# A range test's last step put between two matmul groups, and its result tile allocated ahead of the weights

## The chip, the core and the metric

The kernel runs on one core of a Trainium2 chip. The metric is the device time of one execution in microseconds (us). The kernel before took 517.93 us, the median of three runs (517.24 to 519.18). The execution that the profiler recorded took 517.73 us; its span, from the first to the last instruction, is 516.0 us.

## The reference

The inputs are q, k and v of 4 batches, 8 heads, 768 positions and 64 values a head, two sizes (8 global and 96 local positions), and weights of a feed-forward part that come as float64 numbers. The core of the reference:

```python
scores = scale * np.matmul(q, k.transpose(0, 1, 3, 2)) + bias   # bias falls with the distance
scores = np.where(is_global | is_local, scores, -1e9)
a = np.exp(scores - scores.max(-1, keepdims=True)); a /= a.sum(-1, keepdims=True) + 1e-9
x = np.matmul(a, v)                            # heads joined: (4, 768, 512)
xk = mu_k * x + (1 - mu_k) * x_prev            # x_prev: x one position earlier
xr = mu_r * x + (1 - mu_r) * x_prev
k = np.maximum(xk @ w_k, 0)
out = 1 / (1 + np.exp(-(xr @ w_r))) * (k * k @ w_v)
```

## The kernel before

The rows are cut into 24 tiles of 128 positions. For each tile the kernel makes the scores (tile `s`), the exponentials (`e`), their transposes (`t`, `et`) and the weighted sums (`av`). Two tiles make a chunk of 256 positions for the feed-forward part, of which there are 12. A chunk runs as a generator, `channel_mix`, that the main loop advances by some matmuls at a time, so that TensorE has feed-forward matmuls between the attention's. Each product with a weight is made of three float32r matmuls (`three`, lines 440 to 442), because operands are held as a high and a low part. The groups are `kp` (weights `wk` stationary, 256 columns of `xk` moving; 1152 matmuls), `z` (`xr` stationary, 512 columns of `wr` moving; 288) and `vps` (`kk` stationary, 512 columns of `wv` moving; 576). A chunk ends with two `vps` groups of 24 matmuls. After each of them VectorE multiplies by the sigmoid (line 489) and SyncE issues the write of 128 rows of the output (line 490).

The weights come as 64-bit words and are turned into float32 by bit operations, which hold for a range of exponents only. The kernel therefore loads all weights again in the last two chunks (`range_load`) and tests their exponents (`range_test`): 20 tests, each of which leaves one number per partition in a column of `odd`. At the end, in program order after all chunks, line 554 takes the largest of the 20 columns into `worst[:, 0]`, line 556 turns this column into one row by a product with the identity (`row`), line 557 takes the largest of the row into `worst[0, 1]`, and lines 692 and 693 make of it a flag, `wide_i`. All five engines load the flag into a register (line 695) and branch (line 696). The flag is 0 for these inputs; the branch then leaps over `wide()`, a slow version for all other inputs, to the end of the program. What all engines do from there to the end stands at lines 696 and 738: waits on the DMA counters, resets of semaphores and a barrier.

All tiles of the pool `const` lie one behind the other in the order in which the program allocates them: among others `odd`, `middle`, `k_first`, the ten weight tiles of 8192 bytes per partition (`w0` to `w9`), `worst`, `okf`, `wide_i`. The other pools lie behind it. The pool of the second phase's operands has gaps written in by hand (`GAP`, and the tile `ahead`, which nothing uses), of 64, 448 and 384 bytes per partition.

The order of the instructions on each engine is set by a scheduler that models the time of each; only the order within a queue matters to this case. PSUM tiles of the feed-forward part (`kp`, `z`, `vps`, `row`) share three buffers in turn.

Of the kernel before, what the change touches and what calls it, by code (L numbers as in the profile page):

```python
# [9 lines left out]
F32 = mybir.dt.float32  # L10
# [6 lines left out]
AX = mybir.AxisListType  # L17
# [24 lines left out]
def tile_biased_attention_channel_mix(ctx: ExitStack, tc: tile.TileContext, qT, kT, v, n_sizes, mu_kr, w_k, w_v, w_r, q_rows, k_rows, v_rows, slopes, out):  # L42
    nc = tc.nc
    vec, act, pool, pe = nc.vector, nc.scalar, nc.gpsimd, nc.tensor

    const = ctx.enter_context(tc.tile_pool(name="const", bufs=1))
# [14 lines left out]
    ident = const.tile([128, 128], F32, name="ident")  # L61
# [26 lines left out]
    ps_f = fast.enter_context(tc.tile_pool(name="ps_f", bufs=3, space=PSUM))  # L88
# [108 lines left out]
    words_again, tested = [], [0]  # L197

    def range_load():
        n = len(words_again)  # L200
        if n == 20:
            return
        name, src, j = w_steps[n // 2]
        if n % 2:
            raw = p4k.tile([128, 512, 2], I32, tag="t4k", name=f"again_{n}")
        else:
            raw = q_pool.tile([128, 512, 2], I32, tag=("qh", "ql")[n // 2 % 2], name=f"again_{n}")
        at, o = divmod((j * 2 + n % 2) * 512 // 512 * 1024 + n % 1 * 1024, 2048 if name == "k" else 1024)
        nc.sync.dma_start(raw.rearrange("p n w -> p (n w)"), src[at * 128 : (at + 1) * 128, o : o + 1024])
        words_again.append(raw)  # L210

    def range_test(behind_vec, behind_act):
        n = tested[0]
        if n == len(words_again):
            return
        tested[0] += 1
        raw = words_again[n]
        low, top = raw[:, :, 0], raw[:, :, 1]
        with tc.issue_after(behind_vec.ins):
            vec.tensor_scalar(low, top, 27, 15, op0=ALU.logical_shift_right, op1=ALU.bitwise_and)  # L220
        with tc.issue_after(behind_act.ins):
            act.activation(top.bitcast(F32), low, AF.Abs, bias=middle, accum_out=odd[:, n : n + 1])

    odd = const.tile([128, 20], F32, name="odd")
    middle = const.tile([128, 1], F32, name="middle")
    pool.memset(middle, -7.5)

# [16 lines left out]
    def weights_need(n):  # L244
        weights_go(n, n)
# [172 lines left out]
    def part(pool, tag, n):  # L418
        t = pool.tile([128, n * 256 + GAP.get(tag, 0)], F32R, name=tag, tag=tag)
        return t[:, 0 : n * 256].rearrange("p (a q) -> p a q", a=n)  # L420
# [15 lines left out]
    def channel_mix(xk, xr, out_rows, f_pool, f2_pool, ps_f, more=False):  # L436
        kkh, kkl = (part(f_pool, f"kk_{p}", 8) for p in ("hi", "lo"))

        def three(o, sh, sl, mh, ml, first, last):
            pe.matmul(o, sh, mh, start=first, stop=False)  # L440
            pe.matmul(o, sh, ml, start=False, stop=False)  # L441
            pe.matmul(o, sl, mh, start=False, stop=last)  # L442

        def z_of(i):
            z = ps_f.tile([128, 512], F32, name="z", tag="f")
            c = slice(i * 128, (i + 1) * 128)
            for k in range(4):
                three(z, xr[0][:, k, c], xr[1][:, k, c], *wts["r", k], k == 0, k == 3)
                yield
            sig = f2_pool.tile([128, 512], F32, name="sig", tag="f2")  # L450
            sigs.append((z, sig))

        sigs = []
        for fp in range(4):
            weights_need(4)
            ps = ps_f.tile([128, 512], F32, name="kp", tag="f")
            for u in range(2):
                f = slice((2 * fp + u) * 128, (2 * fp + u + 1) * 128)
                o = ps[:, u * 256 : (u + 1) * 256]
                for k in range(4):  # L460
                    hi, lo = wts["k", k]
                    three(o, hi[:, f], lo[:, f], xk[0][:, k, :], xk[1][:, k, :], k == 0, k == 3)
                    if k % 2:
                        yield
            kk = f2_pool.tile([128, 2, 256], F32, name="kk", tag="f2")
            pv = ps.rearrange("p (a q) -> p a q", a=2)
            act.activation(kk, pv, AF.Relu)  # L467
            vec.tensor_mul(kk, pv, kk)  # L468
            high = act.copy(kkh[:, 2 * fp : 2 * fp + 2, :], kk)  # L469
            rest = vec.tensor_sub(kkl[:, 2 * fp : 2 * fp + 2, :], kk, kkh[:, 2 * fp : 2 * fp + 2, :])  # L470
            if more:
                for i in range(3):
                    range_load()
                for i in range(3):
                    range_test(rest, high)
        weights_need(6)
        for i in range(2):
            yield from z_of(i)
        for z, sig in sigs:
            act.activation(sig, z, AF.Sigmoid)  # L480
        for i in range(2):
            c = slice(i * 128, (i + 1) * 128)
            vp = ps_f.tile([128, 512], F32, name="vps", tag="f")
            sig = sigs[i][1]
            for f in range(8):
                weights_need(7 + f // 2)
                three(vp, kkh[:, f, c], kkl[:, f, c], *wts["v", f], f == 0, f == 7)
                yield
            vec.tensor_mul(sig, vp, sig)
            nc.sync.dma_start(out_rows(i), sig)  # L490

    def ffn(c):
        xt = state["x", c]
        xk = mix(xt[:, :, 1:257], xt[:, :, 0:256], "k", p4k, f_pool, c == 0)
        xr = mix(xt[:, :, 1:257], xt[:, :, 0:256], "r", p4k, f_pool, c == 0)
        return channel_mix(xk, xr, lambda i: out[(2 * c + i) * 128 : (2 * c + i + 1) * 128, :], f_pool, f2_pool, ps_f, c >= 10)
# [53 lines left out]
    while queue:  # L550
        run_ffn(1.0)
    assert tested[0] == 20
    worst = const.tile([128, 2], F32, name="worst")
    vec.reduce_max(worst[:, 0:1], odd, axis=AX.X)
    row = ps_f.tile([128, 512], F32, name="row", tag="f")
    pe.matmul(row[0:1, 0:128], worst[:, 0:1], ident, start=True, stop=True)
    vec.reduce_max(worst[0:1, 1:2], row[0:1, 0:128], axis=AX.X)
    fast.close()


# [16 lines left out]
    def wide():  # L577
        weights_any()
        with ExitStack() as g:
# [85 lines left out]
            with tc.For_i(0, B, 1) as b:  # L665
                for c in range(3):
                    xt = work.tile([128, 4, 257], F32, name="g_x", tag="g_x")
                    src = rows[ds(b, 1)].rearrange("b p a s -> p (b a) s")
                    if c:
                        nc.sync.dma_start(xt, src[:, :, 256 * c - 1 : 256 * c + 256])  # L670
                    else:
                        pool.memset(xt[:, :, 0:1], 0.0)
                        nc.sync.dma_start(xt[:, :, 1:257], src[:, :, 0:256])
                    xk = mix(xt[:, :, 1:257], xt[:, :, 0:256], "k", work, work)
                    xr = mix(xt[:, :, 1:257], xt[:, :, 0:256], "r", work, work)

                    def out_rows(i):
                        return rows_out[ds(b, 1), (2 * c + i) * 128 : (2 * c + i + 1) * 128, :].rearrange("b s d -> (b s) d")

                    for _ in channel_mix(xk, xr, out_rows, work, work4, ps_f):  # L680
                        pass
# [60 lines left out]
```

## Time and profile before

| | |
|---|---|
| three runs | 517.24, 517.93, 519.18 us |
| profiled execution | 517.73 us, span 516.0 us |
| TensorE busy | 503.1 us (98%) |
| VectorE, ScalarE, GpSimd busy | 344.8, 345.8, 220.4 us |
| mean granted TensorE clock | 0.984 of 2.4 GHz |
| data moved | 59.95 MB, 116 GB/s on average |

A page of the profile gives busy time by engine (PE is TensorE's matmuls, PEld its weight loads, DVE is VectorE, ACT ScalarE, POOL GpSimd, SP SyncE). An engine name with a q behind it (SPq, DVEq) is the engine's sequencer, which waits, branches, loads registers and issues DMAs. Matmuls are pipelined: the time from one matmul's start to the next one's start is the pace, and the duration in a row is longer than that.

### The profile page before, as it was taken

Reading aid. Unit: us, or ns where it says so; the run is one execution under the profiler, and the core shown is the slowest. Engines: PE = TensorE matmul, PEld = TensorE weight load, DVE = VectorE, ACT = ScalarE, POOL = GpSimd, SP = SyncE. Lnnn points to the kernel's source line nnn. Section 1 sums busy time; section 2 is a strip of 40 time slices with the busy share of each in tenths; the row PEclk is TensorE's granted clock in tenths of the full one; section 3 lists DMA queues with packets and bytes.
Section 4 is the critical chain, followed back from the end, with each engine's and each line's share of the span. In section 5 each row is a group of like instructions: output and inputs, shape, how many; then the busy total and the mean of one; then the engine's idle time right before and its main releaser. Section 6 shows DMA issues by size and latency. Waiting matters only on the chain.

```text
span 516.0 us, 10305 instructions
## 1 busy us (share of the span) xinstructions
PE 503.1 (98%) x3600; PEld 438.4 (85%) x3600; DVE 344.8 (67%) x837; ACT 345.8 (67%) x857; POOL 220.4 (43%) x368
## 2 busy tenths in 40 slices
PE   6999999999999999999999999999999999999993
PEld 3766998998998998898898998898898998898982
DVE  6897879356388768658678668658678655357330
ACT  4799889567467577567577577567577578596440
POOL 7552434224448445526546535526546515204000
PEclk8799999999999999999999999999999999999997
DMA  8987422304902523603503603603603315567301
GB/s 243 324 221 242 160 85 75 121 1 121 197 20 79 135 69 90 182 8 83 167 13 94 179 10 95 174 12 83 169 13 98 100 27 167 173 204 259 110 0 47
DMA packets 24234, 59.95 MB, mean 116 GB/s; under 512 B 5328, under 2 KB 6352, under 8 KB 23664
## 3 DMA queue, kind: packets, MB, share of 16 engines
q1 hardware_dynamic: 24032, 59.23, 39.9%
q8 instruction: 30, 0.49, 0.4%
q14 instruction: 28, 0.23, 0.2%
q10 hardware_dynamic: 144, 0.00, 0.0%
HBM read 52.93 MB, written 6.29 MB: 115 GB/s over the span
## 4 chain that ended last, share of the span: by engine, by line
PE 96%; DVE 1%; DMA 1%; issue 0%; POOL 0%; DVEq 0%; POOLq 0%
PE kp L440 9%; PE kp L442 9%; PE kp L441 9%; PE vps L440 9%; PE vps L442 9%; PE vps L441 9%; PE av L404 8%; PE t L385 8%; PE z L440 4%; PE z L441 4%; PE z L442 4%; PE s L351 3%; PE s L354 3%; PE s L353 3%; PE s L350 2%; PE rest L188 2%
## 5 line engine op out<-in xcount | busy, mean ns | idle before, releaser
L373 POOL TENSOR_SCALAR e<-e,r 128x232 f32<-128x232 f32 (+1 forms) x180 | 90.4, 520 | 162.4 <-DVE r L367 134.6
L440 PE MATMUL kp<-xk_hi,wk 128*128 128x256 f32 x384 | 109.6, 285 | 0.0
L442 PE MATMUL kp<-xk_hi,wk 128*128 128x256 f32 x384 | 108.5, 283 | 0.0
L441 PE MATMUL kp<-xk_lo,wk 128*128 128x256 f32 x384 | 108.2, 282 | 0.0
L360 ACT ACTIVATE e<-e,nmax 128x232 f32<-128x232 f32 (+1 forms) x192 | 89.9, 472 | 25.8 <-DVE nmax L359 25.0
L359 DVE CUSTOM_DVE_ANT_0 e<-s,pat 128x232 f32<-128x232 f32 (+1 forms) x192 | 64.8, 374 | 31.2 <-PE s L354 16.6
L440 PE MATMUL vps<-wv,kk_hi 128*128 128x512 f32 x192 | 76.3, 398 | 0.0
L441 PE MATMUL vps<-wv,kk_hi 128*128 128x512 f32 x192 | 76.0, 396 | 0.0
L442 PE MATMUL vps<-wv,kk_lo 128*128 128x512 f32 x192 | 76.0, 396 | 0.0
L441 PEld LDWEIGHTS kp<-xk_lo,wk 128*128 128x128 f32 x384 | 72.6, 189 | 0.7 <-issue 0.2
L440 PEld LDWEIGHTS kp<-xk_hi,wk 128*128 128x128 f32 x384 | 72.5, 189 | 0.5
L442 PEld LDWEIGHTS kp<-xk_hi,wk 128*128 128x128 f32 x384 | 72.1, 188 | 0.1
L387 ACT COPY et<-t 128x256 f32<-128x256 f32 (+1 forms) x176 | 56.6, 372 | 12.3 <-PE t L385 11.7
L468 DVE TENSOR_TENSOR kk<-kp,kk 128x512 f32<-128x512 f32 x48 | 33.0, 688 | 43.9 <-ACT kk L467 43.6
L385 PE MATMUL t<-ident,e 128*128 128x128 f32 x352 | 56.0, 279 | 0.0
L470 DVE TENSOR_TENSOR kk_lo<-kk,kk_hi 128x512 fp32r<-128x512 f32 x48 | 35.6, 741 | 22.8 <-ACT kk_hi L469 22.4
L385 PEld LDWEIGHTS t<-ident,e 128*128 128x128 f32 x352 | 41.1, 137 | 11.3 <-issue 2.4
L442 PEld LDWEIGHTS vps<-wv,kk_lo 128*128 128x128 f32 x192 | 36.1, 188 | 8.6
L440 PEld LDWEIGHTS vps<-wv,kk_hi 128*128 128x128 f32 x192 | 36.2, 189 | 7.3
L441 PEld LDWEIGHTS vps<-wv,kk_hi 128*128 128x128 f32 x192 | 36.2, 188 | 7.3
L415 ACT COPY x<-av 128x512 f32<-128x512 f32 x24 | 14.1, 587 | 41.0 <-PE av L404 40.9
L469 ACT CAST kk_hi<-kk 128x512 fp32r<-128x512 f32 x48 | 29.9, 623 | 17.1 <-DVE kk L468 17.0
(113 smaller groups left out, 1108.7 us busy)
## 6 DMA issues: line engine op xcount, KB each, us to landing
qraw<-in_qT_dram SPq DMA_DIRECT2D x32, 256.0 KB
kraw<-in_kT_dram SPq DMA_DIRECT2D x32, 256.0 KB
out_dram<-sig SPq DMA_DIRECT2D x24, 256.0 KB
va<-in_v_dram SPq DMA_DIRECT2D x20, 240.0 KB
vb<-in_v_dram SPq DMA_DIRECT2D x20, 208.0 KB
w<-in_w_k_dram SPq DMA_DIRECT2D x4, 1024.0 KB
w<-in_w_v_dram SPq DMA_DIRECT2D x4, 1024.0 KB
again<-in_w_k_dram SPq DMA_DIRECT2D x8, 512.0 KB
```

Of the source, the lines that this page charges most:

```text
L359: vec.tensor_tensor_reduce(out=e[:, :w], in0=o, in1=p[:, h, :], op0=ALU.add, op1=ALU.min, scale=-0.125, scalar=3.0e38, accum_out=s["nmax"] ...
L360: act.activation(e[:, :w], e[:, :w], AF.Exp, bias=s["nmax"][:, h : h + 1], scale=-1.0, accum_out=s["sum"][:, h : h + 1])
L373: pool.tensor_scalar(e[:, :w], e[:, :w], r[:, u : u + 1], 1.0, op0=ALU.mult, op1=ALU.mult)
L385: pe.transpose(pt[0:p, c : c + 128], e[:, k * 128 : k * 128 + p], ident)
L387: act.copy(et[0:p, k * 256 : k * 256 + 256], pt[0:p, k * 256 : k * 256 + 256])
L404: pe.matmul(o, vt[:, h * 64 : (h + 1) * 64], et[0:p, c + q : c + 128], start=k == 0, stop=k == nb - 1)
L440: pe.matmul(o, sh, mh, start=first, stop=False)
L441: pe.matmul(o, sh, ml, start=False, stop=False)
L442: pe.matmul(o, sl, mh, start=False, stop=last)
L468: vec.tensor_mul(kk, pv, kk)
L469: high = act.copy(kkh[:, 2 * fp : 2 * fp + 2, :], kk)
L470: rest = vec.tensor_sub(kkl[:, 2 * fp : 2 * fp + 2, :], kk, kkh[:, 2 * fp : 2 * fp + 2, :])
```

## The change

`worst` is allocated right behind `odd`, so `middle`, `k_first` and the ten weight tiles lie 32 bytes further on in each partition. The tile that stood behind the weights is gone from there, so that `okf`, `wide_i` and all other pools lie where they lay. The three steps that make `worst` become a function. The last chunk calls it after the first of its two `vps` groups, once all 20 tests are done.

```diff
+    def range_worst():
+        vec.reduce_max(worst[:, 0:1], odd, axis=AX.X)
+        row = ps_f.tile([128, 512], F32, name="row", tag="f")
+        pe.matmul(row[0:1, 0:128], worst[:, 0:1], ident, start=True, stop=True)
+        vec.reduce_max(worst[0:1, 1:2], row[0:1, 0:128], axis=AX.X)
+
     odd = const.tile([128, 20], F32, name="odd")
+    worst = const.tile([128, 2], F32, name="worst")
     middle = const.tile([128, 1], F32, name="middle")
...
             vec.tensor_mul(sig, vp, sig)
             nc.sync.dma_start(out_rows(i), sig)
+            if more and i == 0 and tested[0] == 20:
+                range_worst()
...
     assert tested[0] == 20
-    worst = const.tile([128, 2], F32, name="worst")
-    vec.reduce_max(worst[:, 0:1], odd, axis=AX.X)
-    row = ps_f.tile([128, 512], F32, name="row", tag="f")
-    pe.matmul(row[0:1, 0:128], worst[:, 0:1], ident, start=True, stop=True)
-    vec.reduce_max(worst[0:1, 1:2], row[0:1, 0:128], axis=AX.X)
     fast.close()
```

On VectorE, the end of the program before; `sig_6051` and `sig_6065` are the sigmoids of the last two groups of 128 rows:

```order
L554 TENSOR_REDUCE worst_6122<-odd_174 128x1
L489 TENSOR_TENSOR sig_6051<-vps_6068,sig_6051 128x512
L489 TENSOR_TENSOR sig_6065<-vps_6095,sig_6065 128x512
L557 TENSOR_REDUCE worst_6122<-row_6124 1x1
L692 SCALAR_TENSOR_TENSOR okf_6141<-worst_6122,okf_6141 1x1
L693 CAST wide_i_6142<-okf_6141 1x1
L695 TENSOR_LOAD wide_i_6142
L696 COMPARE_AND_BRANCH
```

And the same place on VectorE now (line numbers are 4 to 7 higher):

```order
L225 TENSOR_REDUCE worst_175<-odd_174 128x1
L496 TENSOR_TENSOR sig_6052<-vps_6069,sig_6052 128x512
L228 TENSOR_REDUCE worst_175<-row_6097 1x1
L696 SCALAR_TENSOR_TENSOR okf_6141<-worst_175,okf_6141 1x1
L697 CAST wide_i_6142<-okf_6141 1x1
L496 TENSOR_TENSOR sig_6066<-vps_6100,sig_6066 128x512
L699 TENSOR_LOAD wide_i_6142
L700 COMPARE_AND_BRANCH
```

The second reduction, the flag's two steps and the cast stand ahead of the last multiplication; the load of the flag and the branch stand behind it as before.

On SyncE, the last rows before the branch, first as they were (the two rows named ISA are register and assertion steps of the flag's load):

```order
L209 DMA again_19_6002<-in_w_v_dram 128x1024
L490 DMA out_0_dram<-sig_6051 128x512
L490 DMA out_0_dram<-sig_6065 128x512
L695 TENSOR_LOAD wide_i_6142
L695 ISA x2
L696 COMPARE_AND_BRANCH
```

And SyncE's rows there now:

```order
L209 DMA again_19_6003<-in_w_v_dram 128x1024
L497 DMA out_0_dram<-sig_6052 128x512
L699 TENSOR_LOAD wide_i_6142
L699 ISA x2
L497 DMA out_0_dram<-sig_6066 128x512
L700 COMPARE_AND_BRANCH
```

The flag's load has moved ahead of the issue of the last write, and the branch follows that issue.

On TensorE, the end of the last group before (`vps_6095` is the last one):

```order
L440 MATMUL vps_6095<-wv3_1074,kk_hi_5884 128x512
L441 MATMUL vps_6095<-wv3_1074,kk_hi_5884 128x512
L442 MATMUL vps_6095<-wv3_1074,kk_lo_5885 128x512
L556 MATMUL row_6124<-ident_62,worst_6122 1x128
L695 TENSOR_LOAD wide_i_6142
L696 COMPARE_AND_BRANCH
```

And on TensorE now, the place where the last but one group (`vps_6069`) ends and the last (`vps_6100`) begins:

```order
L448 MATMUL vps_6069<-wv3_1075,kk_hi_5885 128x512
L449 MATMUL vps_6069<-wv3_1075,kk_lo_5886 128x512
L227 MATMUL row_6097<-ident_62,worst_175 1x128
L447 MATMUL vps_6100<-wv0_662,kk_hi_5885 128x512
L448 MATMUL vps_6100<-wv0_662,kk_hi_5885 128x512
```

The row product has moved from behind the last group to ahead of it; behind the last group the flag's load follows at once. On all engines the order up to these places is that of before.

## Rows read from the trace of the kernel before

**Rows 1.** The page: span, busy time by engine, and the chain's shares by engine.

```profile
span 516.0 us, 10305 instructions
...
PE 503.1 (98%) x3600; PEld 438.4 (85%) x3600; DVE 344.8 (67%) x837; ACT 345.8 (67%) x857; POOL 220.4 (43%) x368
...
PE 96%; DVE 1%; DMA 1%; issue 0%; POOL 0%; DVEq 0%; POOLq 0%
```

**Rows 2.** Stretches: us, busy PE, PEld, DVE, ACT, POOL, PE clock, DMA share, GB/s.

```profile
20.00:60.00 40.00, 40.00 (x272) 29.50 (x272) 36.04 (x88) 37.70 (x100) 17.49 (x20) 1.00 0.71 214
60.00:500.00 440.00, 439.99 (x3233) 392.64 (x3232) 293.55 (x687) 297.43 (x722) 190.30 (x318) 1.00 0.37 104
```

**Rows 3.** Timeline, 495 to 510 us: start, us, engine, line, operation, [idle before].

```profile
496.56 0.18 DVE L554 TENSOR_REDUCE worst<-odd 128x1 f32<-128x20 f32 x1 [0.82 <-ACT again L222]
...
496.71 0.60 ACT L480 ACTIVATE sig<-z 128x512 f32<-128x512 f32 x1 [0.18 <-PE z L442]
...
501.82 0.40 PE L442 MATMUL vps<-wv,kk_lo 128*128 128x512 f32 x1
...
502.05 0.40 PE L440 MATMUL vps<-wv,kk_hi 128*128 128x512 f32 x1
...
507.42 0.40 PE L442 MATMUL vps<-wv,kk_lo 128*128 128x512 f32 x1
...
507.75 0.38 PE L556 MATMUL row<-ident,worst 128*1 128x128 f32 x2
507.93 0.69 DVE L489 TENSOR_TENSOR sig<-vps,sig 128x512 f32<-128x512 f32 x1 [4.98 <-PE vps L442]
...
509.02 0.14 DVE L693 CAST wide_i<-okf 1x1 int32<-1x1 f32 x1
```

**Rows 4.** Lines 490, 695, 696, 738: ns min/median/max, first and last start (us).

```profile
L490 SPq DMA_DIRECT2D out_dram<-sig x2: 343/344/344, 503.0 to 508.6; - x2
...
L695 SPq TENSOR_LOAD <-wide_i x1: 732/732/732, 509.2 to 509.2; - x1
...
L695 DVEq TENSOR_LOAD <-wide_i x1: 839/839/839, 509.2 to 509.2; - x1
...
L696 SPq EVENT_SEMAPHORE  x8: 17/17/17, 514.0 to 514.6; - x8
...
L696 PEldq COMPARE_BRANCH  x1: 3578/3578/3578, 510.1 to 510.1; - x1
...
L696 SPq COMPARE_BRANCH  x1: 50/50/50, 510.6 to 510.6; - x1
...
L696 DVEq EVENT_SEMAPHORE  x1: 21/21/21, 514.2 to 514.2; - x1
...
L738 SPq DRAIN  x3: 7/7/13, 515.1 to 515.5; - x3
```

**Rows 5.** Pace of matmuls: `kp` by timeline, scores by timeline, scores of two tiles grouped.

```profile
484.02 0.28 PE L440 MATMUL kp<-xk_hi,wk 128*128 128x256 f32 x1
...
485.46 0.28 PE L440 MATMUL kp<-xk_hi,wk 128*128 128x256 f32 x1
...
422.83 0.27 PE L353 MATMUL s<-kw,qh 128*128 128x232 f32 x1
422.94 0.27 PE L354 MATMUL s<-kw,ql 128*128 128x232 f32 x1
...
L354 PE MATMUL s<-kw,ql x16: 270/274/280, 402.9 to 438.0; 128*128 128x232 f32 x16
```

**Rows 6.** Timeline: float32 products among float32r matmuls; L351 x2 is one product.

```profile
64.77 0.41 PE L351 MATMUL s<-kz,qz 128*128 128x128 f32 x2
65.01 0.37 PE L350 MATMUL s<-kz,qz 128*128 128x104 f32 x2
...
426.32 0.40 PE L442 MATMUL z<-wr,xr_lo 128*128 128x512 f32 x1
426.65 0.45 PE L404 MATMUL av<-et,va 128*64 128x128 f32 x4
```

## The prediction

> **What bounds the kernel now.** I read the page first, for the engine that is never idle. TensorE is busy 98% of the span and makes 96% of the chain that ended last [rows 1]. The stretches come next, to see whether that holds all along: from 20 to 60 us TensorE is busy 40.00 of 40.00 us, and from 60 to 500 us 439.99 of 440.00, at a granted clock of 1.00 [rows 2]. So in these 480 us only the number and the pace of the matmuls count. What another engine gains or loses there is hidden, unless TensorE has to wait. Last come the timeline of the end and the sequencers' rows, because that is where TensorE no longer covers anything. The last `vps` matmul starts at 507.42 us [rows 3] and the span ends at 516.0 [rows 1]: 8.6 us in which a chain of short steps sets the end.
>
> That chain, step by step. VectorE multiplies from 507.93 to 508.62. Only then come the second reduction, the flag and its cast, which ends at 509.02 + 0.14 = 509.16 [rows 3]. SyncE issued the last write at 508.6 and was done with it 0.34 us later, at 509.0. It then waits for the cast, loads the flag at 509.2 and branches at 510.6. Its first instruction behind the branch runs at 514.0, 3.4 us after the branch. After a list of resets and waits it drains at 515.1 and joins the barrier; the span ends 0.85 us on. VectorE loads the flag at 509.2 and is behind its branch at 514.2, TensorE branches at 510.1 and spends 3.58 us in the branch itself [rows 4]. So SyncE arrives last, some 0.9 us after VectorE.
>
> **The change part by part.** Part one, the row product between the last two `vps`. It is one float32 product of 128 columns. The 128-column float32 product among the scores takes 65.01 − 64.77 = 0.24 us [rows 6]. To go from a float32r matmul to a float32 one with new weights took 426.65 − 426.32 = 0.33 us where the float32r matmul alone paces at 0.23, thus 0.10 more [rows 6]; the same 0.33 us stands ahead of the product in its old place (507.42 to 507.75) [rows 3]. Sum: 0.24 + 0.10 = 0.34 us on TensorE, all of it on the path, since the last group starts later by it. The bounds are 0.24 (the switch is hidden) and 0.24 + 0.33 = 0.57 (nothing of the switch lies beside the matmul ahead). I take 0.34, the sum of the two nearest rows.
>
> It waits for nothing. Its input, the first reduction, is done at 496.56 + 0.18 = 496.74, and the group ahead of it ends its starts at 501.82: 5.1 us to spare. The PSUM buffer that it takes was that of a `z` whose sigmoid was read earlier still; the last group then takes the buffer that the second sigmoid frees at 496.71 + 0.60 = 497.31, 4.7 us ahead of 502.05 [rows 3]. If this cover were gone, every us of it would be one of the end.
>
> Part two, what leaves the end. The second reduction, the flag and the cast now run on VectorE after the first of the last two multiplications, in the 4.98 us that VectorE sits idle there [rows 3]: cost nothing. SyncE loads the flag in the same stretch, behind the issue of the last write but one and ahead of the last. The last write needs the last multiplication, 4 us later, so nothing queued behind the load is late. ScalarE and GpSimd have no more work and branch early.
>
> Part three, the new end. Everything up to the multiplication is 0.34 later: it ends at 508.96, SyncE issues the write at about 509.0 and is done at 509.3, and branches at about 509.4, where it was 510.6. With 3.4 us for the branch and 1.1 for the list behind it, it reaches the barrier at 513.9 to 514.0 where it was 515.1 [rows 4]: 1.2 us earlier. Now VectorE is next in line. Its load of the flag stands behind the last multiplication and can start at about 509.0 (before 509.2), and it was behind the branch 5.0 us after its load began [rows 4], so at 514.0, and 0.1 later it joins. So VectorE and SyncE arrive nearly together, at about 514.05, and the gain is about 1.1, not 1.2. TensorE, 3.58 us in its branch from about 508.9 on, is early. I take 1.15 us.
>
> Part four, the 32 bytes. What moves is the ten weight tiles and two small ones; TensorE reads the weights in every `kp`, `z` and `vps` matmul. As the moving operand, 512 columns at 2.4 GHz would take 213.3 ns, and the pace is (507.42 − 502.05) / 23 = 233.5 [rows 3]. As the stationary operand of 256 columns (106.7 ns) it is (485.46 − 484.02) / 12 = 120.0 [rows 5]. So 20.2 and 13.3 ns a matmul go to something else, and if that is where the operands lie, the shift can take or give. Against it speak the scores in float32r. A head's keys are 232 float32 wide, 928 bytes, and a head's queries 512, so head by head the one moves by 416 bytes against the other, and the two key buffers lie 7424 bytes apart: within 512 bytes two tiles show all sixteen places that are multiples of 32. Their 16 matmuls of line 354 last 270 to 280 ns [rows 5], and the pace is 422.94 − 422.83 = 0.11 us throughout. A place that cost 7 ns would show. I cost the shift at nothing. The bounds on both sides are the difference of the two excesses, 20.2 − 13.3 = 6.9 ns, on the 288 + 576 matmuls that move weights: 6.0 us less or more. As for loading and splitting the weights, that lies below the 480 us in which TensorE never waits [rows 2].
>
> One rule bears on the excess. The Trainium skill, TensorE: Matmul & The Clock Gate, section "Wait — 56ns, not 53.3ns?", gives the start-to-start time of a warm matmul as its columns at 2.4 GHz and some 2.5 ns: 215.8 at 512 columns, where this trace has 233.5. By that page 17.7 ns of each would be a loss that could be had back, on 864 matmuls 15.3 us, and the estimate would be 501 us if the shift did so. The skill's SBUF — State Buffer, section "Who interferes with whom", says that TensorE never waits on another's access to the memory. By that rule the place changes nothing, and the sixteen places above agree.
>
> **The sum.** Against the profiled execution's own 517.73: −1.15 gives 516.6 us; the 0.34 is in it already. With the product at 0.24 it is 516.5, at 0.57 it is 516.8. The profiled execution lies 0.2 below the median of the three runs, whose spread is 1.9.
>
> **Rivals.** First, the end stays where it was, only later. Three engines are held up behind the branch, and all three are back between 513.7 and 514.2 though they branched 0.5 us apart [rows 4]; SyncE's branch would now fall right on the last write, 0.4 us after its issue began, where it used to lie 2 us behind. If the return is set by a common transfer and not by each branch, the gain goes and the product stays: 517.73 + 0.34 = 518.1. Against it: 3.4 to 4.1 us after each branch is a narrow range.
>
> The Trainium skill, Runtime: NRT & Kernel Launch, section "Instruction fetch mechanics", says that a taken branch to a page outside the window of two waits for a transfer of that page. By that rule the wait starts at each engine's own branch, as the forecast has it; TensorE's 3.58 us inside the branch agree, and no row here shows which transfer is whose.
>
> Second, on the other side: the weights' new place slows their matmuls. The mechanism is TensorE reading a moving operand while it loads the next stationary one: `wr` and `wv` stream while `xr` and `kk` are loaded, and only the first two move. Should the two now meet in the same part of the memory, each matmul pays. At 6.9 ns on 864 matmuls that is 516.6 + 6.0 = 522.6 us. It decides from (520.5 − 516.6) / 864 = 4.5 ns a matmul on. For it: the 20.2 ns, which no wait in the trace explains. Against it: the sixteen places.
>
> Third, the same with the other sign: the two meet now and no longer do, 516.6 − 6.0 = 510.6 us. The evidence is the same. That the whole excess goes is the far end of this case.
>
>
>
> **How the numbers follow.** Under 0.5%, 2.6 us, a measurement of this kernel cannot tell from no change: 515.3 to 520.5 around 517.93. Forecast 516.6: 0.66. End not moved, 518.1: 0.17. Slower weights, 522.6: 0.09. Faster weights, 510.6: 0.08. The first two lie within 0.5%, but for 0.03 in which a quick chip shows the forecast as faster. So faster 0.11, the same 0.80, slower 0.09. The range takes the forecast and the unmoved end with the spread of the runs, 1 us or a little more either side: 515.0 to 519.2, which leaves out the two cases of the weights and some of the edges.
>
> **What would show it.** In the new trace the starts of the last two `vps` groups should be parted by about 0.57 us where they were 0.23, and VectorE's last multiplication should begin 0.3 later. SyncE's branch should come about 0.5 us after the write's issue begins, and the span should end 7.0 to 7.2 us after the last matmul's start (before 8.6). The paces should be 233.5 and 120.0 ns again. The forecast is wrong if either pace differs by more than a nanosecond, if SyncE is behind its branch no earlier than 514.0, or if a wait appears at the row product.

## The result, and the profile after

The changed kernel takes 509.03 us, the median of four runs (508.92 to 511.49), against 517.69 before (517.24 to 519.18, four runs): a ratio of 0.9839, 95% interval 0.9803 to 0.9875. The forecast was 516.6, its range 515.0 to 519.2. The time lies 6 us below the range, near the third rival's 510.6, which had a chance of 0.08.

The page of the changed kernel, which answers to [rows 1]:

```profile
span 507.2 us, 10304 instructions
...
PE 495.6 (98%) x3600; PEld 434.4 (86%) x3600; DVE 342.9 (68%) x837; ACT 345.0 (68%) x857; POOL 221.5 (44%) x368
```

Its stretches, which answer to [rows 2]:

```profile
20.00:60.00 40.00, 38.84 (x258) 28.35 (x257) 33.56 (x82) 35.84 (x95) 15.17 (x20) 1.00 0.75 215
60.00:500.00 440.00, 440.00 (x3255) 394.50 (x3254) 294.14 (x691) 296.92 (x722) 192.65 (x318) 1.00 0.36 104
```

TensorE is as gapless from 60 to 500 us as before and at the same clock, but fits 3255 matmuls into the stretch where there were 3233. With the same work, no wait gone and no step of the clock, the matmuls themselves must be quicker. Their starts show it. First 24 steps of `kp`, then the last `vps` group from its 11th to its 24th matmul, 13 steps. The timeline of before (start, us, instruction), whose last `vps` is in [rows 3]:

```profile
479.70 0.28 PE L440 MATMUL kp<-xk_hi,wk 128*128 128x256 f32 x1
...
482.58 0.28 PE L440 MATMUL kp<-xk_hi,wk 128*128 128x256 f32 x1
...
504.39 0.40 PE L441 MATMUL vps<-wv,kk_hi 128*128 128x512 f32 x1
```

The timeline of after:

```profile
476.11 0.28 PE L449 MATMUL kp<-xk_hi,wk 128*128 128x256 f32 x1
...
478.94 0.28 PE L449 MATMUL kp<-xk_hi,wk 128*128 128x256 f32 x1
...
498.43 0.39 PE L448 MATMUL vps<-wv,kk_hi 128*128 128x512 f32 x1
...
501.38 0.39 PE L449 MATMUL vps<-wv,kk_lo 128*128 128x512 f32 x1
```

A `vps` took (507.42 − 504.39) / 13 = 233 ns and takes (501.38 − 498.43) / 13 = 227; a `kp` took 120.0 and takes 2.83 / 24 = 117.9. Over the whole trace the paces were 119.9 (`kp`), 233.2 (`z`) and 233.3 ns (`vps`) and are 117.7, 230.0 and 228.8. Here and below such a pace is the mean of the steps from one matmul to the next of its kind, without the two to four in a hundred that are longer than 150 ns (`kp`) or 260 ns (`z`, `vps`) because of a break. Times their counts this is, as an estimate, 1152 × 2.2 + 288 × 3.2 + 576 × 4.5 ns = 2.5 + 0.9 + 2.6 = 6.0 us.

Most of the rest is the end. Its timeline, which answers to [rows 3]:

```profile
495.40 0.39 PE L449 MATMUL vps<-wv,kk_lo 128*128 128x512 f32 x1
495.71 0.09 PEld L227 LDWEIGHTS row<-ident,worst 128*1 128x1 f32 x2 [0.35 <-issue]
495.71 0.38 PE L227 MATMUL row<-ident,worst 128*1 128x128 f32 x2
495.82 0.69 DVE L496 TENSOR_TENSOR sig<-vps,sig 128x512 f32<-128x512 f32 x1 [5.29 <-PE vps L449]
496.02 0.19 PEld L447 LDWEIGHTS vps<-wv,kk_hi 128*128 128x128 f32 x1 [0.22 <-issue]
496.02 0.50 PE L447 MATMUL vps<-wv,kk_hi 128*128 128x512 f32 x1
...
496.36 0.39 PE L448 MATMUL vps<-wv,kk_hi 128*128 128x512 f32 x1
...
496.92 0.14 DVE L697 CAST wide_i<-okf 1x1 int32<-1x1 f32 x1
...
501.87 0.69 DVE L496 TENSOR_TENSOR sig<-vps,sig 128x512 f32<-128x512 f32 x1 [4.82 <-PEq L700]
```

The row product stands between the last two groups, whose neighbouring starts are 496.02 − 495.40 = 0.62 us apart, where a step is 0.23: 0.39 more. The step behind it is slow too, 496.36 − 496.02 = 0.34, 0.11 more. So the product costs 0.50 us, and nothing waits for data there ("issue"). The flag is ready at 497.06, 4.8 us ahead of the last multiplication. The sequencers from there on, which answer to [rows 4] (ns min/median/max, first and last start):

```profile
L497 SPq DMA_DIRECT2D out_dram<-sig x24: 343/373/1094, 91.9 to 502.6; - x24
...
L699 SPq TENSOR_LOAD <-wide_i x1: 737/737/737, 497.1 to 497.1; - x1
...
L699 DVEq TENSOR_LOAD <-wide_i x1: 543/543/543, 501.9 to 501.9; - x1
...
L700 SPq EVENT_SEMAPHORE  x8: 17/17/17, 503.5 to 505.8; - x8
...
L700 PEldq COMPARE_BRANCH  x1: 3462/3462/3462, 498.2 to 498.2; - x1
...
L700 DVEq COMPARE_BRANCH  x1: 72/72/72, 502.5 to 502.5; - x1
L700 SPq COMPARE_BRANCH  x1: 50/50/50, 503.0 to 503.0; - x1
L700 DVEq EVENT_SEMAPHORE  x1: 21/21/21, 505.7 to 505.7; - x1
...
L742 SPq DRAIN  x3: 7/7/13, 506.4 to 506.7; - x3
```

SyncE branches at 503.0 and goes on at 503.5: 0.5 us, where it took 3.4 before (510.6 to 514.0 [rows 4]). Its eight resets, however, now stretch over 2.3 us (before 0.6). What holds it is in its waits (who waits for whom, us in all, times, longest):

```profile
SPq L700 <- SPq L700: 2.3, 2, 1.9
```

The 1.9 us end at the reset of the counter that the last write of the output raises, at 505.56, 2.96 us after that write's issue began. VectorE is behind its branch at 505.7, 3.1 us after it (before 4.1). So two new waits end almost together, and the span ends 507.23 − 501.38 = 5.85 us after the last `vps` matmul's start instead of 515.96 − 507.42 = 8.54. Less 0.50 for the product (above), the end gives 2.2 us. With the paces: 6.0 + 2.2 = 8.2 of the 8.7 us between the two profiled executions (517.73 and 509.01).

The other 0.5 us comes, as I read it, from the start of the two executions and not from the change. The granted clock there was 0.84 on average from 0 to 12 us and 0.59 from 12 to 20 before, and 0.98 and 0.82 after; in a second profile of the same changed kernel (`i2` below) it was 0.85 and 0.59. Part of the quicker start is lost again from 20 to 60 us, where TensorE is busy 38.84 us after (above) and 40.00 in i2. What is left shows in `e1` below, which has the paces of before, up to its last two groups also the order of before, and 0.98 and 0.82 at the start. The first `vps` matmul of the last chunk before, in e1 and after:

```profile
496.45 0.40 PE L440 MATMUL vps<-wv,kk_hi 128*128 128x512 f32 x1
```

```profile
495.82 0.40 PE L450 MATMUL vps<-wv,kk_hi 128*128 128x512 f32 x1
```

```profile
490.18 0.39 PE L447 MATMUL vps<-wv,kk_hi 128*128 128x512 f32 x1
```

Of the changed kernel's 6.3 us up to there, e1 has 0.6 without a change of pace. The other 5.6 are the paces, to which the last two groups add some 0.3.

### The profile page after: what moved, and what is told of

It is laid out like the page before. It is cut to its first block, busy times and chain, and to the rows that moved or that the text cites. A ratio compares the mean times of both kernels' runs of the same rounds, so it can differ in the third digit from the quotient of the medians.

```text
span 507.2 us, 10304 instructions
## 1 busy us (share of the span) xinstructions
PE 495.6 (98%) x3600; PEld 434.4 (86%) x3600; DVE 342.9 (68%) x837; ACT 345.0 (68%) x857; POOL 221.5 (44%) x368
## 5 line engine op out<-in xcount | busy, mean ns | idle before, releaser
L380 POOL TENSOR_SCALAR e<-e,r 128x232 f32<-128x232 f32 (+1 forms) x180 | 89.2, 514 | 162.2 <-DVE r L374 125.4
L447 PE MATMUL vps<-wv,kk_hi 128*128 128x512 f32 x192 | 75.6, 395 | 0.0
L448 PE MATMUL vps<-wv,kk_hi 128*128 128x512 f32 x192 | 75.0, 391 | 0.0
L411 PE MATMUL av<-et,va 128*64 128x128 f32 x384 | 40.4, 282 | 0.0
```

Source lines behind the costliest of these rows:

```text
L380: pool.tensor_scalar(e[:, :w], e[:, :w], r[:, u : u + 1], 1.0, op0=ALU.mult, op1=ALU.mult)
L411: pe.matmul(o, vt[:, h * 64 : (h + 1) * 64], et[0:p, c + q : c + 128], start=k == 0, stop=k == nb - 1)
```

## The experiments

Starts are given in bytes of a partition. Before, modulo 512, a weight tile starts at 288, `kk` and `xr` at 320, `xk` at 384; the high and the low part of an operand have the same start modulo 256. The change puts the weights at 320. What the text calls a distance is the start of the moving operand less that of the stationary one, modulo 256: for `vps` and `z` that of the weights less that of `kk` or `xr`, for `kp` that of `xk` less that of the weights. Before, the distances are 224 and 96, after 0 and 64. In the expectations theory A is that the place of the operands against each other sets the pace, B and C that each operand's own start does (multiples of 64 bytes are quick), D and E are forms of A and C in coarser steps.

**The two halves of the change.** The first kernel moves only the product, with `worst` allocated in its old place among the tiles; the second moves only `worst`.

```diff
 # e1_product_only: range_worst() behind the first of the last two vps groups
+        worst = const.tile([128, 2], F32, name="worst")   # inside range_worst(), behind the weights
 # e2_shift_only: the product stays at the end
+    worst = const.tile([128, 2], F32, name="worst")       # behind odd
```

> Only the row product is moved between the last two vps groups; the weights stay where they were before. Theory (two separate gains): the paces stay at 233.5 ns for 512 moving columns and 120.0 ns for kp, and only the end shrinks: the span ends 5.8 to 5.9 us after the last matmul's start instead of 8.5, less 0.33 us for the product, so 517.7 - 2.4 = 515.3 us, ratio 0.995. Rival (the order of the program, not the place of the weights, changed the pace): the pace of the vps matmuls is 227 and the time is 509 us, ratio 0.983.

> Only the tile is allocated ahead of the weights (weights 32 bytes further on); the row product stays at the end. Theory (two separate gains): the vps pace falls to 227 to 229 ns, kp to 118, the last vps group starts 6 us earlier than before and the end stays 8.5 us long: 511.4 us, ratio 0.988. Rival (order, not place): paces of 233.5 and 120.0, no change, 517.7 us, ratio 1.000.

The product alone gives 514.97 us, ratio 0.9954 (0.9926 to 0.9983), 2.4 us, with the paces of before (119.9, 233.3, 233.2). By the times alone it could be anything from 0.9 to 3.8 us; the trace agrees with the 2.4: the span ends 5.67 us after the last `vps` matmul's start, where it was 8.54, and the product costs 0.5. The shift alone gives 511.19, ratio 0.988 (0.9814 to 0.9945), 6.2 us, with the paces of after (117.7, 230.1, 228.7). The product of the two ratios is 0.9835: the halves add up to the whole.

**Is it the weights' place or the distance?** The next kernels move the second phase's operands as well (`ahead` lies in front of them, a tile `pad` in front of the weights).

```diff
 # e3_both_plus32: e2, and                  # e4_phase2_plus32: before, and
-    f_pool.tile([128, 96], F32, name="ahead", tag="ahead")
+    f_pool.tile([128, 104], F32, name="ahead", tag="ahead")
 # e6_all_plus64: after, and
+    const.tile([128, 16], F32, name="pad")
 # e5_weights_plus64: after, with the pad, and ahead 80 for 96
```

> The weights and the second phase's operands (kk, xk, xr and what lies behind them) are both 32 bytes further on; the row product stays at the end. Theory A (what counts is the place of the two operands against each other): as before, 233.5 and 120.0 ns, 517.7 us, ratio 1.000. Theory B (what counts is that a moving operand of 512 columns starts on a multiple of 64 bytes by itself): wr and wv do, so z and vps pace at 227 to 229 ns as with the shift alone, kp no better than 120 since xk no longer starts on a multiple of 64: 513 to 514 us, ratio 0.992.

> The weights stay where they were before; the second phase's operands lie 32 bytes further on. Theory A (place of the operands against each other): weights against kk and xr stand as in the changed kernel, so z and vps pace at 227 to 229 ns and the time is about 511 to 513 us, ratio 0.990. Theory B (a moving operand's own start): wr and wv still start 32 bytes off a multiple of 64, and xk now does too: 233.5 ns for vps and z, kp 120 or more, 517.7 us or more, ratio 1.000 or above.

> The changed kernel with the weights 64 bytes further on again (96 in all); the second phase's operands stay. Theory C (a float32r matmul is slowed if its moving or its stationary operand starts off a multiple of 64 bytes, and nothing else counts): both still start on multiples of 64, paces as in the changed kernel, 228.8 ns for vps and 117.7 for kp, 509.0 us, ratio 0.983. Theory D (the two operands' places against each other count at steps of 64 bytes too, and the changed kernel happens to sit well): the paces move by 2 ns or more, the time to 504 or to 515.

> The changed kernel with everything from the weights on 64 bytes further on, so that weights, kk and xr start on multiples of 128. Theory C: 228.8 and 117.7 ns, 509.0 us, ratio 0.983. Theory D: the same, since the places against each other are the same. A third theory E (multiples of 128 are better than of 64): vps near 226.7 ns throughout and kp near 113, 502 us.

With weights and operands both 32 bytes on, the whole gain is gone: 517.69 us, ratio 0.9997 (0.9972 to 1.0023), paces 119.8, 232.8, 233.1. The same 13 steps of `vps` in that kernel take 3.04 us:

```profile
504.04 0.40 PE L442 MATMUL vps<-wv,kk_hi 128*128 128x512 f32 x1
...
507.08 0.40 PE L443 MATMUL vps<-wv,kk_lo 128*128 128x512 f32 x1
```

With everything 64 on (e6) the gain stays: 509.5, ratio 0.9837 (0.9813 to 0.9861), paces 117.8, 229.8, 228.4. For e4, 516.58, ratio 0.9975 (0.9945 to 1.0004), paces 119.0, 233.2, 233.5, the expectation had the sign of the move wrong: the distance of `vps` becomes 192, not 0. In e5 (distances 64 and 0) `vps` paces at 229.9 and `kp` at 119.6: 511.96, ratio 0.9893 (0.9866 to 0.992). There the weights alone moved, still lie at a multiple of 64, and all the same `kp` lost what it had gained.

**Single operands and whole distances.** The gaps in front of `xk` and `xr` make any pair of distances, with weights and all else in place. The kernels are the one after but for these lines:

```diff
 # (ahead, gap 1, gap 2) in floats     after: 96, 16, 112
-GAP = {"kk_hi": 16, "xk_lo": 112}
+GAP = {"kk_hi": 0, "xk_lo": 0}         # e7_no_gaps, ahead 96
+GAP = {"kk_hi": 24, "xk_lo": 104}      # e8_xk_plus32, ahead 96
+GAP = {"kk_hi": 64, "xk_lo": 64}       # f1_128_128, ahead 64
+GAP = {"kk_hi": 0, "xk_lo": 128}       # f2_256_256, ahead 32
+GAP = {"kk_hi": 64, "xk_lo": 64}       # f3_384_384, no ahead
+GAP = {"kk_hi": 32, "xk_lo": 96}       # f4_448_192, ahead 112
```

> The changed kernel without the two gaps written by hand (GAP set to 0): kk, xk and xr and the weights all start at the same place within 512 bytes, all on multiples of 64. Theory C: 509.0 us, paces as in the changed kernel, ratio 0.983. Theory D: the pace of kp moves, since xk alone stood elsewhere before; a collision at one place would make it slower, 512 us or more.

> The changed kernel with xk alone 32 bytes further on. Theory C: only kp, whose moving operand xk is, loses its gain: 119.8 ns instead of 117.7 on 1152 matmuls, 2.4 us, so 511.4 us, ratio 0.988; z and vps stay at 230.0 and 228.8. If z and vps slow down too, the pace is not set by the two operands of the matmul itself.

> The changed kernel with other gaps, so that within 512 bytes the weights start 128 bytes behind kk and xr (0 before) and xk starts 128 bytes behind the weights (64 before); all on multiples of 64. Theory C (only the multiple of 64 counts) and the changed kernel's 509.0 us: ruled out by e5 and e7 already if kp or vps differs again. Theory D (the place of the moving against the stationary operand counts in steps of 64 bytes): kp somewhere in 113 to 120 ns and vps in 227 to 233 ns, constant over the chunks; e5 and e7 gave kp 119.6 at a distance of 0 and the changed kernel 117.7 at 64. If more distance is better, kp at 115 and 506 us; if 64 is the best place, kp 120 and 512 us.

> As f1, with distances of 256 and 256 bytes: the two operands half of 512 bytes apart. Theory D with a period of 256 or less: like the distance 0, kp 119.6 and vps 228.7, 511 us. Theory D with a period of 512: the best place, kp 113 and vps 227, 502 us.

> As f1, with distances of 384 and 384 bytes. Theory D with a period of 128: kp as at 0, 119.6 ns, vps 228.7, 511 us. With a period of 256: as in f1. With a period of 512: a number of its own.

> As f1, with the weights 448 bytes behind kk and xr, and xk 192 bytes behind the weights. Theory D with a period of 128: kp as at 64, 117.7 ns, and vps as in e5 (distance 64), 229.9 ns: 509.6 us. Otherwise numbers of their own.

| kernel | us | ratio, 95% interval | `kp`, `z`, `vps` ns |
|---|---|---|---|
| e7 | 511.31 | 0.9877 (0.9852 to 0.9901) | 119.7, 229.9, 228.7 |
| e8 | 511.91 | 0.9895 (0.9867 to 0.9923) | 119.9, 230.2, 228.7 |
| f1 | 513.74 | 0.994 (0.992 to 0.9961) | 119.0, 232.6, 232.9 |
| f2 | 511.07 | 0.9869 (0.9848 to 0.9889) | 119.7, 229.9, 228.7 |
| f3 | 513.84 | 0.9931 (0.9907 to 0.9956) | 119.0, 232.7, 232.9 |
| f4 | 511.09 | 0.9864 (0.9841 to 0.9887) | 114.9, 233.1, 233.4 |

In e8 only `xk` moves, and only `kp` changes. f1 and f3 differ by 256 bytes in both distances and agree within 0.1 ns, as e7 and f2 do; so the table can be read modulo 256. f4 has the quickest `kp` so far and the `vps` of before.

**Distance or own start, and the best pair.** All kernels up to here that had quick `vps` also had the weights and `kk` at multiples of 64. The first of the next four has the distances of after and no operand at such a multiple; it is the kernel before but for one line. The others are the kernel after with other gaps.

```diff
+    f_pool.tile([128, 88], F32, name="ahead", tag="ahead")   # h1_before_minus32: 88 for 96
+GAP = {"kk_hi": 48, "xk_lo": 80}       # h2_0_192, ahead 96
+GAP = {"kk_hi": 64, "xk_lo": 64}       # h3_32_224, ahead 88
+GAP = {"kk_hi": 64, "xk_lo": 64}       # h4_96_160, ahead 72
```

> The kernel before with ahead at 88 floats for 96: kk, xr and xk lie 32 bytes nearer, the weights stay, the product stays at the end. Starts modulo 256 bytes: weights 32, kk and xr 32, xk 96, so the distances (moving less stationary) are those of the kernel after, 0 for vps and z and 64 for kp, but no operand starts at a multiple of 64. Theory of the distance: paces as after, kp 117.7, z 230.0, vps 228.7 ns, so 517.6 - 6.0 = 511.5 us, ratio 0.988. Rival, the weights' own start (multiples of 64 are quick): paces as before, 119.9, 233.2, 233.3 ns, 517.6 us, ratio 1.000.

> The kernel after with gaps of 192 and 320 bytes for 64 and 448: xk alone moves by 128, so that its distance from the weights is 192 (modulo 256), where f4 had its quickest kp, and that of vps and z stays 0. Theory of the distance: kp 114.9, z 230.0, vps 228.7 ns; 1152 x 2.8 = 3.2 us below the kernel after, 505.8 us, ratio 0.977 to before. Rival, that f4's quick kp came from its slow vps or from another place: kp 117.7 or more, 509 us or more, ratio 0.984 or above.

> The kernel after with ahead 352 bytes and gaps of 256 and 256: distances 32 for vps and z and 224 for kp, both not tried so far. Theory of the distance, a straight line between the neighbours: vps 229.3, z 230.1 ns (0 gives 228.7 and 230.0, 64 gives 229.9 and 230.2), kp 117.3 (192 gives 114.9, 0 gives 119.6); 509.1 us, ratio 0.984. Rival, only distances that are multiples of 64 are quick: vps 233, z 233, kp 120 ns as before, 515.2 us, ratio 0.995.

> The kernel after with ahead 288 bytes and gaps of 256 and 256: distances 96 for vps and z and 160 for kp, both not tried so far. Theory of the distance, a straight line between the neighbours: vps 231.4, z 231.4 ns (64 gives 229.9 and 230.2, 128 gives 232.9 and 232.6), kp 117.0 (128 gives 119.0, 192 gives 114.9); 510.2 us, ratio 0.986. Rival, only distances that are multiples of 64 are quick: vps 233, z 233, kp 120 ns, 515.2 us, ratio 0.995.

h1, eight floats fewer in a tile that nothing uses, has the paces of after to a tenth (117.7, 230.1, 228.7) and takes 512.15 us, ratio 0.9901 (0.9881 to 0.9922). The own start falls. Its 13 steps of `vps` and 24 of `kp` take 2.94 and 2.83 us:

```profile
476.15 0.28 PE L442 MATMUL kp<-xk_hi,wk 128*128 128x256 f32 x1
...
478.98 0.28 PE L442 MATMUL kp<-xk_hi,wk 128*128 128x256 f32 x1
...
499.00 0.39 PE L441 MATMUL vps<-wv,kk_hi 128*128 128x512 f32 x1
...
501.94 0.39 PE L442 MATMUL vps<-wv,kk_lo 128*128 128x512 f32 x1
```

h2 puts the two best distances together: 507.32 us, ratio 0.981 (0.9794 to 0.9827), paces 115.5, 230.1, 228.7. The gain over the kernel after is smaller than the 3.2 us expected, since `kp` reached 115.5 and not 114.9: at distance 192 each stretch of `kp` matmuls without a break settles, after some five steps, at one of two levels, 113 or 118 ns, and h2 has more of the second. In its trace 23 steps of the quick level, 2.60 us or 113 ns each:

```profile
370.11 0.28 PE L447 MATMUL kp<-xk_hi,wk 128*128 128x256 f32 x1
...
372.71 0.28 PE L449 MATMUL kp<-xk_hi,wk 128*128 128x256 f32 x1
```

h3 takes 514.11 us, ratio 0.9945 (0.9929 to 0.9962), with 118.3, 233.2, 233.1; h4 513.19, ratio 0.9919 (0.99 to 0.9937), with 118.1, 233.6, 233.6. For both the straight line between the neighbours failed for `vps` and `z`: 32 and 96 are as slow as before, though 0 and 64 are quick. The rival failed for `kp`, which has 118 at 160 and 224.

**Period and best pair.** h2 with `ahead` at 32 floats, so that all operands lie 256 bytes nearer; beside it on the same chip the kernel after, unchanged.

> h2 with all operands of the second phase 256 bytes nearer: distances 256 for vps and z and 448 for kp, which modulo 256 are h2's 0 and 192. Theory of a period of 256 bytes: the paces of h2, kp 115.5, z 230.1, vps 228.7 ns, 507.3 us, and 2 us (1152 x 2.2 ns = 2.5 us, less what the clock takes) below the kernel after on the same chip. Rival, a period of 512: kp or vps differ from h2 by over 1.5 ns, 509 us or more, no quicker than the kernel after.

> The kernel after unchanged, beside i1 on the same chip, since its first four runs spread over 2.6 us: kp 117.7, z 230.0, vps 228.8 ns and 509.0 to 509.5 us, ratio 0.984, if its first measurement and that of h2 hold; 507.5 us or less if h2's lead was one of the chip.

i1 has the paces of h2 (115.5, 230.1, 228.7) and 507.38 us, ratio 0.9815 (0.9793 to 0.9838); the kernel after has 117.7, 230.2, 228.8 and 509.96, ratio 0.986 (0.9835 to 0.9885). So the period is 256 at the distances tried, and the pair 0 and 192 is 2.6 us quicker than the kernel after in the medians of one chip, 2.5 of them worked out from `kp` (1152 × 2.2 ns); the two intervals just touch.

All runs in one table, ns from start to start by distance (modulo 256 bytes; a dash was not tried):

| distance | 0 | 32 | 64 | 96 | 128 | 160 | 192 | 224 |
|---|---|---|---|---|---|---|---|---|
| `vps` | 228.7 | 233.1 | 229.9 | 233.6 | 232.9 | – | 233.4 | 233.3 |
| `z` | 230.0 | 233.2 | 230.2 | 233.6 | 232.6 | – | 233.1 | 233.2 |
| `kp` | 119.6 | – | 117.7 | 119.9 | 119.0 | 118.1 | 114.9 to 115.5 | 118.3 |

## Why the prediction was wrong

**Part four failed, the 32 bytes.** The step was "A place that cost 7 ns would show. I cost the shift at nothing." It read the place's cost from the scores, whose 16 places pace at 0.11 us throughout [rows 5]. But these steps cannot show it. In two tiles the scores have 128 moving columns and not 232. A group of four there, and the first two of a group with 232:

```profile
220.59 0.30 PE L353 MATMUL s<-kw,qh 128*128 128x128 f32 x1
220.73 0.28 PE L354 MATMUL s<-kw,ql 128*128 128x128 f32 x1
220.84 0.28 PE L353 MATMUL s<-kw,qh 128*128 128x128 f32 x1
220.95 0.27 PE L354 MATMUL s<-kw,ql 128*128 128x128 f32 x1
...
422.52 0.36 PE L353 MATMUL s<-kw,qh 128*128 128x232 f32 x1
422.72 0.28 PE L354 MATMUL s<-kw,ql 128*128 128x232 f32 x1
```

From the second matmul of a group on the step is 0.11 us with 128 columns and with 232 [rows 5]: it is not set by the moving columns, and I conclude that what a place costs the moving operand can have room below it. The first step of a group does go by the columns, 0.14 and 0.20 us, so "throughout" was not true either. Whether the scores hide such a cost or have none stays open, since no run moves their two operands against each other. An argument from what a probe doesn't show needs a probe without slack, and these rows, which were there to be read, say that this one had some. The bounds drawn from the two excesses, 6.0 us either way, were of the right size.

**The third rival** had sign and size (6.0 us; the shift alone gave 6.2). Its mechanism, a moving operand read while the next stationary one is loaded, fits the finding that the distance of just these two counts. But it does not say why `vps` is quickest where the two starts coincide (distance 0, 228.7 ns) and `kp` nearly slowest there (119.6). No run looks inside TensorE, so it isn't shown. Its sum came out partly by chance: it took 6.9 ns on the 864 matmuls that move weights, which got 0.9 + 2.6 = 3.5 us, and nothing for `kp`, which got 2.5. That the second rival, the same with the other sign, was given the higher chance had no ground; among the distances tried, the place of before was near the slow end.

By the Trainium skill, SBUF — State Buffer, "Who interferes with whom", TensorE never waits on another's access to the memory, and the prediction took the place to change nothing by it. That sentence speaks of other engines, and no run here contradicts it. TensorE's own two operands, which it does not cover, cost or save up to 5 ns a matmul by where they start. The rule of the Trainium skill's TensorE: Matmul & The Clock Gate, "Wait — 56ns, not 53.3ns?", comes to 215.8 ns for 512 columns; no distance tried here reached it, and the lowest mean was 228.4 (e6).

**Part one was right in kind.** Nothing waits for the product. It costs 0.50 us where 0.34 was forecast, within the bounds of 0.24 and 0.57: the sum had a term for going into float32, and none for the slow step back (0.11).

**Part two was right.** The flag's steps run beside the last group. SyncE loads the flag at 497.1 and is back in time for the last write.

**Part three had the mechanism, and its size was off.** The step was "With 3.4 us for the branch and 1.1 for the list behind it". e1 has it apart from the rest: 2.4 us, where 1.15 was forecast. The 3.4 us did not move with the branch, they went, and only part came back as the wait for the last write, which the prediction had not priced because it was long done before. It goes by the order and not by the places. In all five profiles with the product at the end (before, e2, e3, e4, h1) SyncE goes on 3.4 to 3.7 us after its branch, and the span ends 8.5 to 8.8 us after the last `vps` matmul's start; in all fifteen with the product between the groups it is 0.49, and 5.6 to 6.2.

The wait for the last write is also longer than that write used to take. Before, it was counted as done 2.04 us after its issue began, and after 2.95. What was moved while it ran, before (508.6 to 510.7 us) and after (502.6 to 505.6 us), by queue and kind (packets, MB, share; "instruction" is the page's word for transfers of code):

```profile
q1 hardware_dynamic: 144, 0.26, 32.7%
```

```profile
q1 hardware_dynamic: 144, 0.26, 23.4%
q14 instruction: 2, 0.02, 2.4%
```

The first of the two code transfers starts at 503.60, 1.1 us after VectorE's branch. In all fifteen profiles with the new order code is moved while the last write runs, and the write takes 2.7 to 3.3 us; in all five with the old order none is, and it takes 2.0. No run moves these transfers alone, so that they make the write longer is not shown.

What I can read of the cause of SyncE's short branch is a correlation too. The transfers of code came in a bunch just behind the branches before (511.0 to 511.6 us) and 3.5 us ahead of SyncE's branch after (498.9 to 499.5 us). The two stretches, before and after (queue, kind: packets, MB, share):

```profile
q14 instruction: 4, 0.03, 15.1%
q8 instruction: 1, 0.02, 12.9%
```

```profile
q14 instruction: 3, 0.02, 13.6%
q8 instruction: 1, 0.02, 11.5%
```

The second bunch follows the branches of ScalarE and GpSimd at 497.9 and TensorE's at 498.2. Whether one of its transfers served SyncE stays open; no run took it apart. Against it stands VectorE's branch at 502.5, behind the same bunch, which still took 3.1 us.

**Rival one**, an end that doesn't move, falls with e1. Of the signs named beforehand, the starts 0.57 apart (0.62) and SyncE's branch 0.5 behind the issue (0.4) came; the paces of 233.5 and 120.0 and the end 7.0 to 7.2 us after the last matmul (5.8) did not.

## What to carry to other kernels

Where TensorE has no gap, read the pace from start to start against what the columns would take; an excess that no wait explains may hang on where the two operands start relative to each other, and a few bytes in an unused tile try it out. An edit that adds or drops a small tile ahead of large ones is also an edit of all distances behind it, so move the tile alone before crediting the rest. Before "the trace shows no effect" is used as evidence, look for the row that says whether the effect could have shown.

## What the runs showed that was not expected

- The pace of float32r matmuls depends on the distance of the two starts with a period of 256 bytes, 228.7 to 233.6 ns at 512 moving columns and 114.9 to 119.9 at 256. The best distance for the one (0) is among the slowest for the other.
- At distance 192 `kp` has two levels, 113 and 118 ns. A stretch without a break keeps the level at which it settled, and the next one, also of the same group, can have the other. Why is open, as are distances 160 for `vps` and 32 for `kp`.
- From its taken branch to its next instruction SyncE took 3.4 to 3.7 us in every profile with the product at the end, and 0.49 in every one with the product ahead of the last group.
- The last write of 256 KB took 2.0 us in the first kind of profile and 2.7 to 3.3 in the second, where code is moved beside it and the program's end waits for it.
